# A new order for the last three quarters of the steps of an SSD and SwiGLU kernel

## The chip, the cores and the metric

The kernel runs on one core of a Trainium2 chip. The metric is the device time of one execution in microseconds, the median of several runs. The engines are PE (TensorE; its weight loads are listed apart as PEld), DVE (VectorE), ACT (ScalarE), POOL (GpSimd) and SP (SyncE, which issues most DMAs).

## The reference

A chunked linear attention (Mamba2's SSD) is followed by an RMS norm and a SwiGLU feed-forward network, all in fp32. There are 4 sequences of 768 tokens with 8 heads of width 32 and a state of 16; together they are 3072 tokens of width 256 for the network, whose hidden width is 1536.

```python
for c in range(nc):                                  # chunks of 32
    cum = np.cumsum(la, axis=-1)
    L = np.exp(cum[:, :, :, None] - cum[:, :, None, :]) * causal
    CB = np.einsum('bhin,bhjn->bhij', Cc, Bc)
    y_intra = np.einsum('bhij,bhjd->bhid', CB * L, xc)
    y_inter = np.einsum('bhin,bhnd->bhid', Cc, state) * decay_to_i[:, :, :, None]
    y[:, :, sl] = y_intra + y_inter
    Bx = np.einsum('bhjn,bhjd->bhjnd', Bc, xc) * decay_from_j[:, :, :, None, None]
    state = decay_full[:, :, None, None] * state + np.sum(Bx, axis=2)
...
rms = np.sqrt(np.mean(x * x, axis=-1, keepdims=True) + 1e-06)
xn = x / rms * rms_g
g = xn @ w_gate
silu = g * (1.0 / (1.0 + np.exp(-g)))
return (silu * (xn @ w_val)) @ w_out
```

## The kernel before

**Blocks.** The tokens are worked on in six blocks of 512, numbered 0 to 5. While the network of one block runs on PE, the SSD of the next block is computed between its matmuls. A step's first number is the block in whose stretch it stands; the steps of the SSD in that stretch work for the block after it.

**The network of a block.** Gate and value products are formed by seven products instead of eight (P.1 to P.7, L951 in `product_gv`, for each of six slices j of the hidden width), each of two matmul instructions of 128x256. They are summed up in two PSUM banks, gate and val, of which there are two each. Between them ACT copies the gate bank to SBUF (`take`, L957, tile p), DVE adds such a copy to the value bank (`C`, L963, tile c), ACT takes the silu (`silu`, L208, in place on c, or from gate to u) and DVE or POOL multiplies the halves (`hid` and `hidp`, L976). The product with w_out is a scheme of twenty products (O.0 to O.19, L1072) on sums of hidden tiles (`u` on DVE, `up` on POOL, L1046, tile s); DVE and ACT gather the results into the output tile ob (`w`, L1103 and L1099), and SP stores it (`put`, L1108). Block 0 is simpler: its output product is L983 (step `o`), its results are copied by ACT in `put` (L1114).

**The SSD of the next block.** DVE transposes B and C (`T`, L544), ACT masks them (`Tt`, L1180), PE forms the products CB (`g`, L599), which DVE multiplies with L (`L`, `L1`, L632); L comes from a DMA of log decays, exponentials on ACT (`ex`, L208) and a causal mask on POOL. PE then makes the outputs y (`y`, L736) and the state's additions (L664), DVE updates the states (`S`, L688). For the norm ACT squares y (`sq`) and copies it (`yt`, L804 and L807), PE takes the mean (`ms`, L820), ACT the root by Ln and Exp (`rs`), the roots go out to DRAM and come back on all partitions (`rb`), and DVE scales y to xn (`xn`, L847; `tx`, `txp`: differences for the seven products).

**What sets the order.** The kernel holds one list of 1667 steps, written out as text (from L1269). A loop at its end (L1458 and after) runs through the list and calls the function of each step. Nothing is reordered behind it: each engine executes its own instructions in the order in which the list issues them, and waits where an operand or a buffer isn't ready. Most buffers are few: gate, val, u and L have two each, p and c four, xn, yt, sq and ob one. In PSUM, g shares banks with the output o of block 0.

**Function sets on ACT.** Silu is in one set of functions, Exp and Ln in another. `functions` (L193) remembers the set that the list has loaded last, and emits a load (L200 for silu, L202 for exp and ln) only where a step needs the other one:

```python
        if loaded[0] != name:
            loaded[0] = name
            if name == "silu":
                nc.scalar.preload_act_table(AF.Silu)
            else:
                nc.scalar.preload_act_table_set("natural_log_exp_and_others")
```

A silu, an exponential or a logarithm calls it, and so do two steps by themselves: `table` (silu) and `exps` (exp).

Of the kernel before, what the change touches and what calls it, by code (L numbers as in the profile page):

```python
# [20 lines left out]
def kernel(  # L21
# [35 lines left out]
    P = 128  # L57
    NB, NH, S, D = x.shape
# [5 lines left out]
    T = NB * S  # L64
# [790 lines left out]
    hid = const.tile([P, NF, 2, 256], FP32, name="hid")  # L855
# [383 lines left out]
    def of_chunk(n, fn):  # L1239
# [82 lines left out]
        1:take.6.4 1:P.1.5 1:take.1.5 0:table.0 1:C.11.5 1:P.2.4 1:silu.11.5 1:C.11.4 1:silu.12.2
        1:scale2.1 1:hid.12.2 1:P.7.4 1:P.6.5 1:take.7.4 1:silu.11.4 1:sq2.1.1 1:sq2.0.3 1:sq2.1.2
        2:dT.1 1:P.5.4 1:sq2.0.2 3:bc.1 1:take.6.5 1:two.9 1:Td.0 1:P.4.4 1:hid.11.4 1:sq2.0.0
        1:C.22.4 1:twop.6 1:silu.22.2 1:hid.22.2 1:sq2.0.1 2:dT.0 1:hid.11.5 1:sq2.1.3 1:g
        1:silu.21.4 1:silu.22.4 1:hid.21.4 1:hidp.22.4 1:P.7.5 1:O.15.0 1:P.5.5 1:L1.3 1:L 1:L1.2
        1:u.0 1:take.7.5 1:P.4.5 1:O.2.0 1:O.2.1 1:y.0 1:C.22.5 1:P.3.5 1:silu.21.5 1:w.0 1:hid.21.5
        1:u.1 1:u.2 1:O.15.1 1:O.3.0 1:up.3 1:O.0.0 1:O.0.1 1:up.4 1:O.3.1 1:C.12.5 1:silu.22.5
        1:silu.12.5 2:S.0 1:hid.12.5 1:O.16.0 1:O.6.0 1:O.16.1 1:w.2 1:up.5 1:up.6 1:w.4 1:O.4.0
        1:P.3.4 1:w.10 1:u.9 1:O.4.1 1:O.17.0 1:C.12.4 1:O.9.0 2:T.0.1 1:w.3 1:hid.22.5 1:x.1  # L1330
        1:O.9.1 1:silu.12.4 1:hid.12.4 1:O.17.1 2:Tt.0.0 1:w.12 1:w.5 1:y.1 1:u.10 1:up.11 1:u.7
        1:w.6 1:O.18.0 2:T.1.1 0:exps 2:S.1 1:sq 1:O.13.0 1:O.13.1 1:O.8.0 1:O.8.1 1:w.11 1:w.13
        1:w.20 2:spread.3 2:spread.1 2:sq2.1.0 1:w.16 2:T.1.0 1:yt 1:O.11.0 1:O.18.1 1:w.9 1:ms 1:rs
# [12 lines left out]
        2:take.7.3 2:take.7.2 2:silu.12.1 3:S.0 2:sq2.1.3 2:sq2.0.1 2:spread.0 2:sq2.1.1 3:T.1.1
        2:hid.11.3 2:hid.22.1 2:P.5.2 2:P.5.3 3:Tt.1.1 2:C.22.2 2:C.22.3 2:P.4.3 3:Tt.1.0 3:Td.1
        2:silu.22.3 2:silu.21.3 2:hid.21.3 2:x.1 2:y.1 3:S.1 2:sub.1 2:sq2.0.3 2:hidp.12.1 2:subp.2
        2:P.4.2 2:sq2.0.2 3:dT.0 2:silu.22.2 2:table 2:hidp.22.3 2:sq 2:P.1.5 2:silu.21.2 2:hid.21.2
        1:put.1 3:spread.3 2:P.3.2 3:T.0.0 2:C.12.2 2:take.1.5 2:yt 2:P.3.3 3:T.1.0 3:T.0.1 2:C.12.3  # L1350
        2:hid.22.2 2:P.1.4 2:P.2.5 2:P.6.5 2:silu.12.2 3:Tt.0.1 2:take.1.4 2:silu.12.3 3:Tt.0.0
        2:subp.0 2:hidp.12.3 2:take.6.5 2:hidp.12.2 2:C.11.5 2:P.6.4 2:silu.11.5 3:spread.0 4:dT.0
        2:take.6.4 2:P.2.4 2:C.11.4 2:silu.11.4 3:bc.0 3:subp.0 2:P.7.5 2:take.7.5 2:P.7.4 2:P.5.4
        2:hid.11.5 3:Td.0 2:take.7.4 2:P.4.5 2:C.22.4 2:silu.22.4 2:silu.21.5 2:hid.11.4 2:hid.21.5
        2:P.4.4 2:silu.21.4 2:hid.21.4 3:spread.2 3:subp.2 2:P.5.5 3:sq2.1.3 3:sq2.0.0 3:sq2.0.1
        3:sq2.0.3 3:sq2.1.1 2:ms 2:rs 3:sq2.1.2 2:O.2.0 2:O.15.0 2:hidp.22.4 2:C.22.5 2:P.3.5
        2:C.12.5 2:up.1 2:O.0.0 2:u.2 2:O.2.1 2:O.0.1 2:u.9 2:O.15.1 2:up.0 2:ex.1 2:u.3 2:O.6.0
        2:silu.12.5 2:silu.22.5 2:hid.22.5 2:w.2 2:P.3.4 2:O.16.0 3:sq2.0.2 2:C.12.4 2:w.0
        2:hid.12.5 2:rb 2:xn 2:O.16.1 2:O.3.0 2:w.3 2:O.17.0 2:O.3.1 2:O.4.0 2:O.6.1 2:w.1 2:O.17.1
        2:silu.12.4 2:w.5 2:w.4 2:w.10 3:scale2p.0 2:up.4 2:up.5 3:exps 3:g 3:x.0 2:tx.2 2:txp.0  # L1360
        3:P.1.0 2:tx.1 2:O.9.0 2:O.9.1 2:O.4.1 3:sq2.1.0 2:w.6 2:w.11 2:ex.0 2:exps 3:take.1.0
        3:P.6.0 3:P.2.0 3:C.11.0 2:up.6 2:hidp.12.4 2:up.7 2:w.12 2:O.18.0 2:O.18.1 2:w.9 3:take.6.0
        2:ex.2 2:up.8 2:O.8.0 2:u.10 2:w.7 2:w.13 2:O.8.1 3:P.5.0 2:w.16 2:w.8 3:P.7.0 3:silu.11.0
# [114 lines left out]
```

## Time and profile before

| | |
|---|---|
| median of three runs | 388.94 us (388.43, 388.94, 390.91) |
| span of the profiled execution, the time that its page gives | 387.3 us |
| busy: PE, DVE, ACT, POOL | 381.6, 268.5, 213.6, 149.9 us |
| loads of a function set on ACT | 20 of 1.283 us |
| first instruction that the new order moves | at about 90 us |

Busy time of PE counts a matmul until its modelled end, which lies behind the start of the next one, so a busy share of 99% still leaves room for short waits; the distance between the starts of matmuls, and what the weight loads (PEld) waited for, show these. In a timeline a row is start, length, engine, line, operation, tiles and count; the bracket says how long the engine idled before it, and for whom. "issue" is a wait for nothing that the profile shows.

### The profile page before, as it was taken

The page shows a single profiled execution, that of the slowest core. Times are in us where ns is not written, and L with a number is a line of the kernel's source. Part 1 is how long each engine was busy: PE and PEld are TensorE (multiplying, and loading weights), DVE is VectorE, ACT ScalarE, POOL GpSimd, SP SyncE. Part 2 cuts the span into 40 slices and gives each one's busy share as a digit, 9 for nine tenths or more (in the row PEclk, how much of TensorE's full clock was granted, in tenths as well). Part 3 has the DMA queues.
Part 4 walks back from the last instruction along what each step waited for, and adds up shares of the span by engine and source line. Part 5 has one row for each costly group of instructions (what it writes and reads, how often), then busy time and mean ns, then how long its engine had stood idle before and what let it go on. Part 6 is the DMA issues. An engine that isn't in the chain of part 4 may idle for free.

```text
span 387.3 us, 9593 instructions
## 1 busy us (share of the span) xinstructions
PE 381.6 (99%) x3805; PEld 328.9 (85%) x3805; DVE 268.5 (69%) x593; ACT 213.6 (55%) x451; POOL 149.9 (39%) x168
## 2 busy tenths in 40 slices
PE   8999999999999999999999999999999999999996
PEld 5675488888888989888899988899888899988996
DVE  7886889897636897869475756677474475545674
ACT  3777778978734263578764245742646552245420
POOL 5022145528551463425669401364722046113131
PEclk9999999999999999999999999999999999999999
DMA  7888996588125415534550101001000010000001
GB/s 90 244 129 250 293 192 151 136 134 114 28 67 60 59 50 89 119 54 102 73 96 17 54 15 30 0 16 47 29 3 3 2 34 29 29 1 0 2 0 56
DMA packets 109940, 28.04 MB, mean 72 GB/s; under 512 B 94824, under 2 KB 107848, under 8 KB 109896
## 3 DMA queue, kind: packets, MB, share of 16 engines
q1 hardware_dynamic: 107816, 27.30, 33.8%
q8 instruction: 30, 0.49, 0.6%
q10 hardware_dynamic: 2080, 0.13, 0.4%
q14 instruction: 14, 0.11, 0.1%
HBM read 23.68 MB, written 3.74 MB: 71 GB/s over the span
## 4 chain that ended last, share of the span: by engine, by line
PE 94%; DVE 2%; DMA 2%; issue 1%; ACT 0%; SPq 0%; DVEq 0%
PE gate L951 30%; PE o L1072 23%; PE val L951 22%; PE o L983 5%; PE y L736 3%; PE gate L865 3%; PE g L599 2%; DMA rowe<-e_sb 1%; PE e L460 1%; DMA dT<-rowe 1%; PE gate L875 1%; PE g L592 1%; PE y L664 1%; PE tp L540 1%; PE e L474 0%
## 5 line engine op out<-in xcount | busy, mean ns | idle before, releaser
L963 DVE TENSOR_TENSOR c<-val,p 128x512 f32<-128x512 f32 x99 | 67.3, 688 | 57.5 <-PE val L951 32.7
L957 ACT COPY p<-gate 128x512 f32<-128x512 f32 x99 | 57.2, 582 | 55.6 <-PE gate L951 55.1
L951 PE MATMUL gate<-tx,wgv 128*128 128x256 f32 x264 | 65.9, 381 | 0.0
L976 POOL TENSOR_TENSOR hid<-c 128x256 f32<-128x256 f32 x31 | 24.3, 785 | 94.1 <-ACT c L208 87.5
L208 ACT ACTIVATE c<-c 128x256 f32<-128x256 f32 x99 | 40.6, 416 | 35.8 <-DVE c L963 35.6
L951 PEld LDWEIGHTS gate<-tx,wgv 128*128 128x128 f32 x264 | 49.4, 190 | 7.1 <-issue 0.3
L1072 PE MATMUL o<-two,hid 128*128 128x128 f32 x280 | 38.7, 275 | 0.0
L1103 DVE TENSOR_TENSOR ob<-ob,o 128x128 f32<-128x128 f32 (+1 forms) x90 | 24.0, 299 | 19.9 <-PE o L1072 15.5
L1072 PEld LDWEIGHTS o<-two,hid 128*128 128x128 f32 x280 | 35.6, 192 | 0.7 <-issue 0.2
L976 DVE TENSOR_TENSOR hid<-c 128x256 f32<-128x256 f32 x68 | 30.6, 460 | 7.2 <-ACT c L208 6.8
L951 PE MATMUL val<-tx,sw 128*128 128x256 f32 x132 | 34.0, 382 | 0.0
L951 PE MATMUL val<-xn,sw 128*128 128x256 f32 x132 | 33.6, 381 | 0.1
L951 PE MATMUL val<-xn,wgv 128*128 128x256 f32 x132 | 33.6, 381 | 0.0
L951 PE MATMUL gate<-xn,wgv 128*128 128x256 f32 x132 | 33.2, 381 | 0.0
L951 PE MATMUL gate<-tx,sw 128*128 128x256 f32 x132 | 32.6, 379 | 0.0
L951 PEld LDWEIGHTS val<-tx,sw 128*128 128x128 f32 x132 | 24.6, 190 | 3.9 <-issue 0.4
L951 PEld LDWEIGHTS val<-xn,wgv 128*128 128x128 f32 x132 | 24.8, 190 | 3.4
L208 ACT ACTIVATE u<-gate 128x256 f32<-128x256 f32 (+1 forms) x37 | 14.9, 405 | 22.9 <-PE gate L951 19.3
L951 PEld LDWEIGHTS gate<-tx,sw 128*128 128x128 f32 x132 | 24.8, 190 | 3.2
L951 PEld LDWEIGHTS gate<-xn,wgv 128*128 128x128 f32 x132 | 24.5, 190 | 3.5 <-DVE xn L847 0.2
L951 PEld LDWEIGHTS val<-xn,sw 128*128 128x128 f32 x132 | 24.4, 190 | 3.3 <-DVE c L963 0.2
L1046 POOL TENSOR_TENSOR s<-hid 128x512 f32<-128x512 f32 x13 | 17.3, 1330 | 22.6 <-DVE hid L976 16.2
(202 smaller groups left out, 703.8 us busy)
## 6 DMA issues: line engine op xcount, KB each, us to landing
L<-rowd SPq DMA_DIRECT2D x32, 128.0 KB, 3.3
xr<-in_x_dram SPq DMA_DIRECT2D x24, 128.0 KB, 3.5
out_dram<-ob SPq DMA_DIRECT2D x24, 128.0 KB, 1.8
wr<-in_moe_w_out_dram SPq DMA_DIRECT2D x6, 511.5 KB, 4.9
wr<-in_moe_w_gate_dram SPq DMA_DIRECT2D x5, 511.5 KB, 4.4
wr<-in_moe_w_val_dram SPq DMA_DIRECT2D x5, 511.5 KB, 5.0
br<-in_B_dram SPq DMA_DIRECT2D x23, 64.0 KB, 3.1
dT<-rowe SPq DMA_DIRECT2D x10, 128.0 KB
```

Source lines behind the costliest of these rows:

```text
L208: nc.scalar.activation(**operands)
L599: nc.tensor.matmul(out=g[u, P * i:P * i + P].rearrange("p (t m) -> p t m", t=2), lhsT=T[r, i, 0, u], rhs=T[r, i, 1:3, u], start=(first and ...
L736: nc.tensor.matmul(out=y[2 * k + u][rows, (2 * n + i) * HC:(2 * n + i + 1) * HC], start=(k, u, rows.start) not in opened, stop=True, skip_ ...
L865: nc.tensor.matmul(out=gv[:, k], lhsT=w[:, t, fs], rhs=xns[0][:, t], start=(t == 0), stop=(t == 1))
L951: nc.tensor.matmul(out=dst[:, half[w]], lhsT=lhsT, rhs=rhs, start=(k in (1, 2, 5) and w == 0), stop=True, skip_group_check=True)
L957: nc.scalar.copy(out=t, in_=Xs[j])
L963: nc.vector.tensor_tensor(out=t, in0=Zs[j], in1=a, op=ALU.add)
L976: engine.tensor_tensor(out=hid[:, 2 * j + c // 10 - 1, c % 10 - 1], in0=u, in1=src[:, half[1]], op=ALU.mult)
L983: nc.tensor.matmul(out=o, lhsT=hid[:, f, k // 2, (k % 2) * P:(k % 2 + 1) * P], rhs=wo[:, f], start=opens, stop=(f == NF - 1), skip_group_c ...
L1046: engine.tensor_tensor(out=hidden_or_sum(o), in0=hidden_or_sum(in0), in1=hidden_or_sum(in1), op=ALU.add if in1[0] == "+" else ALU.subtract)
L1072: nc.tensor.matmul(out=Os[blk, b][:, place * P:(place + 1) * P], lhsT=hidden_or_sum(u)[:, g], rhs=rhs, start=(blk, b) not in opened, stop= ...
L1103: nc.vector.tensor_tensor(out=o, in0=o, in1=src, op=ALU.add if what[0] == "+" else ALU.subtract)
```

## The change

From the 400th step on the list is in another order. No step is added or left out. The text of the list becomes one line longer, so lines behind it move by one. The first 399 steps, which prepare the weights and run block 0 up to its network's second half, stay. The diff replaces 131 lines by 132; the first of them are these, with the two places that the order below shows:

```diff
@@ -1307,131 +1307,132 @@
         0:man.16 1:P.2.0 1:C.11.1 1:P.6.1 1:take.6.1 1:P.6.0 1:silu.11.1 1:take.6.0 1:C.11.0
         1:silu.11.0 0:o.5 0:wt.16 1:spread.3 0:sq2.2.1.0 1:sub.3 1:hid.11.1 0:tx.1.3 0:hidgp.22.5
         1:ex.3 0:ex.10 0:sub.8 1:cw.2.1 1:cwp.2.3 1:P.7.0 0:ex.11 1:take.7.0 1:P.5.0 1:C.22.0
-        1:P.7.1 1:P.5.1 1:P.4.0 1:take.7.1 1:twop.1 0:sq2.2.0.3 0:sq2.2.1.1 0:sq2.2.1.2 1:C.22.1
-        1:T.1.1 1:T.0.1 1:P.4.1 1:silu.22.0 1:Tt.1.0 1:silu.21.1 1:bc.1 1:spread.1 1:bc.0
...
-        1:C.22.4 1:twop.6 1:silu.22.2 1:hid.22.2 1:sq2.0.1 2:dT.0 1:hid.11.5 1:sq2.1.3 1:g
...
-        3:P.1.0 2:tx.1 2:O.9.0 2:O.9.1 2:O.4.1 3:sq2.1.0 2:w.6 2:w.11 2:ex.0 2:exps 3:take.1.0
...
+        1:sq2.0.3 1:sq2.0.2 0:put.0 2:bc.0 1:sq2.0.0 1:sq2.1.2 1:spread.1 0:put.2 1:P.3.3 1:P.1.4
+        1:take.1.4 1:g 1:C.12.3 1:silu.12.3 1:hidp.12.3 1:twop.4 1:hidp.12.1 1:twop.7 1:twop.6
...
+        3:P.5.1 3:C.22.1 3:P.1.4 3:silu.22.1 3:hid.22.1 3:P.6.3 3:take.6.3 2:exps 3:take.1.4
+        3:silu.22.0 3:hid.11.1 3:y.1 3:P.2.3 3:hid.11.0 3:sub.3 3:C.11.3 3:P.3.1 3:C.12.1
...
```

PE ahead of the step g that stands in block 1's stretch, in the order before (gate and val are the network's products, o the output of block 0, g the SSD's):

```order
L951 MATMUL gate<-tx,wgv 128x256 x2
L951 MATMUL gate<-tx,sw_992 128x256 x2
L951 MATMUL val<-tx,sw_793 128x256 x2
L951 MATMUL gate<-tx,wgv 128x256 x2
L599 MATMUL g<-T 64x128 x4
```

and now:

```order
L951 MATMUL gate<-tx,wgv 128x256 x4
L983 MATMUL o<-wo,hid 128x256 x4
L951 MATMUL val<-xn,sw_783 128x256 x2
L951 MATMUL gate<-xn,wgv 128x256 x2
L599 MATMUL g<-T 64x128 x4
```

The last matmuls of block 0's output, which stood further ahead, are now four matmuls in front of g.

ACT around the four copies of that output (L1114), before:

```order
L957 COPY p<-gate 128x512
L208 ACTIVATE c<-c 128x256
L1114 COPY ob<-o 128x256 x4
L208 ACTIVATE u<-gate 128x256
L208 ACTIVATE c<-c 128x256
L208 ACTIVATE u<-gate 128x256
```

and now:

```order
L208 ACTIVATE u<-gate 128x256
L957 COPY p<-gate 128x512
L1180 ACTIVATE T<-T,tmask 128x2x128
L208 ACTIVATE c<-c 128x256
L1180 ACTIVATE T<-T,tmask 128x2x128
L1114 COPY ob<-o 128x256 x4
L957 COPY p<-gate 128x512
```

Ahead of the copies there are now two masks, a copy of gate and two silus in a row.

ACT in block 3's stretch, where the step exps of block 2 stands. Before, its load (L202) came ahead of the exponentials of L:

```order
L202 ACT_TABLE_LOAD
L208 ACTIVATE L<-L 128x512
L957 COPY p<-gate 128x512
L1099 COPY ob<-o 128x128
L208 ACTIVATE ob<-o 128x128
L957 COPY p<-gate 128x512
L208 ACTIVATE L<-L 128x512
L200 ACT_TABLE_LOAD
```

and now, where the two exponentials have come earlier and a silu has intervened:

```order
L202 ACT_TABLE_LOAD
L208 ACTIVATE L<-L 128x512 x2
L957 COPY p<-gate 128x512 x2
L200 ACT_TABLE_LOAD
L208 ACTIVATE u<-gate 128x256
L208 ACTIVATE c<-c 128x256 x2
L957 COPY p<-gate 128x512
L208 ACTIVATE c<-c 128x256
L957 COPY p<-gate 128x512
L202 ACT_TABLE_LOAD
L957 COPY p<-gate 128x512
L200 ACT_TABLE_LOAD
```

The step exps loads the exponentials' set once more, and a silu loads its own back behind a single copy; in the whole program the loads are 20 before and 24 now.

243 lines of the change are left out of this document (122 added, 121 removed).

## The prediction

> **What bounds the kernel now.** I read the page's busy line and chain first, then the table by windows, then the waits of PE's weight loads from the place of the change on.
>
> ```profile
> span 387.3 us, 9593 instructions
> PE 381.6 (99%) x3805; PEld 328.9 (85%) x3805; DVE 268.5 (69%) x593; ACT 213.6 (55%) x451; POOL 149.9 (39%) x168
> PE 94%; DVE 2%; DMA 2%; issue 1%; ACT 0%; SPq 0%; DVEq 0%
> ```
>
> PE is busy for 99% of the span and carries 94% of the chain that ended last. The windows say whether that is so stage by stage (columns: length, then busy time and instructions of PE, weight loads, DVE, ACT, POOL, then clock, DMA share and GB/s):
>
> ```profile
> 100.00:120.00 20.00, 20.00 (x94) 17.62 (x93) 9.48 (x20) 8.50 (x20) 8.27 (x10) 1.00 0.31 57
> 340.00:360.00 20.00, 20.00 (x95) 17.60 (x94) 9.50 (x18) 10.51 (x24) 4.37 (x6) 1.00 0.00 0
> ```
>
> In these stretches PE has no idle time, and ACT, the engine on which the change adds something, is busy 8.50 and 10.51 of 20 us. A busy PE can still hide short gaps under the modelled ends of its matmuls, so the stricter view is what the weight loads waited for from 90 us, where the new order begins, to the last matmul (what waited, for whom, us in total, times, longest):
>
> ```profile
> PEld y L736 <- issue: 1.3, 4, 0.3
> PEld ms L820 <- issue: 1.0, 3, 0.3
> PEld o L1072 <- issue: 0.8, 4, 0.2
> PEld g L599 <- issue: 0.7, 2, 0.3
> PEld val L951 <- DVE c L963: 0.6, 2, 0.3
> PEld gate L951 <- issue: 0.5, 3, 0.2
> PEld y L736 <- DVE hid L976: 0.3, 1, 0.3
> PEld o L1072 <- DVE s L1046: 0.3, 1, 0.3
> PEld gate L951 <- DVE xn L847: 0.2, 1, 0.2
> PEld val L951 <- issue: 0.2, 1, 0.2
> ```
>
> The waits on another engine add up to 0.6 + 0.3 + 0.3 + 0.2 = 1.4 us in five places. The issue waits, 1.3 + 1.0 + 0.8 + 0.7 + 0.5 + 0.2 = 4.5 us, stand where PE turns from large matmuls to the small ones of g, y and ms. Nothing waits for a table load or for a DMA. So an order alone can gain at most 1.4 us, 0.4% of the time; what it can lose is open.
>
> **The change part by part.** *PE's own work.* All 1980 matmuls stay, and from 90 us on their shapes are the same in another order: nothing to gain or lose. Turns from one kind of matmul to another are 145 in the order before and 142 now, counted along PE; at up to 0.3 us a turn that is between -0.9 us and 0. I take 0, because most turns are between gate/val and output products, which show almost no issue wait.
>
> *What goes.* The five waits sit at pairs of steps that no longer follow each other in the same way, so I let all of them go: -1.4 us.
>
> *Table loads.* Which function set ACT holds follows from the order of the steps, and a load is emitted only where it differs. Counted along ACT, the old order has 20 loads, the new one 24: not every instruction is kept as it was, four are added.
>
> ```profile
> L202 ACT ACT_TABLE_LOAD x10 | 12.8, 1283 | 0.9 <-PEq L1462 0.8
> L200 ACT ACT_TABLE_LOAD x10 | 12.8, 1283 | 0.2
> 89.09 1.17 ACT L957 COPY p<-gate 128x512 f32<-128x512 f32 x2
> 90.28 1.28 ACT L200 ACT_TABLE_LOAD   x1
> 91.57 0.42 ACT L208 ACTIVATE c<-c 128x256 f32<-128x256 f32 x1
> ```
>
> 4 x 1.283 = 5.13 us more on ACT, which is busy 213.6 of 387 us. What a load costs PE is set by what is queued behind it: the copies of gate (p) that PE needs before it may overwrite the bank, and the silus that DVE's products need. The 20 loads of before stand in the same traffic and no row names one as waited for, so the lower bound is 0; the upper is 5.13. Two of the added loads form a pair with one copy of gate between them (amid block 3's products, where the step exps stands between two takes) and no exponential; there ACT does 1.28 + 0.58 + 1.28 us in a row, and I price what comes through at 0.15 us. At two more places a load now stands directly ahead of the exponentials that a due product needs: an output product whose totals DVE must take first (0.25), and the y of the next block, which waits for L (0.1). Sum 0.5 us, near the lower end, where the 20 rows are.
>
> The row of 90.28 bears on a rule of the Trainium skill, "ScalarE: Activation LUTs", section "What ACT_TABLE_LOAD costs": a load costs about 2.7 us, the drain before it included. By that figure the four loads would be about 10.7 us of ACT. The trace disagrees: the copies end at 89.09 + 1.17 = 90.26, and the silu begins at 91.57, 1.31 us later.
>
> *The place of g.* The step g of block 2 (the small products that feed L) comes earlier and now stands right behind the four copies of the first block's output, which empty the banks g writes into.
>
> ```profile
> 112.92 1.20 ACT L1114 COPY ob<-o 128x256 f32<-128x256 f32 x4 [1.69 <-PE o L983]
> 124.04 1.21 PE L599 MATMUL g<-T 32*64 32x128 f32 x64
> 340.31 1.03 PE L951 MATMUL gate<-tx,wgv 128*128 128x256 f32 x4
> 341.18 1.03 PE L951 MATMUL gate<-xn,wgv 128*128 128x256 f32 x4
> L208 ACT ACTIVATE u<-gate 128x256 f32<-128x256 f32 x33 | 12.5, 382 | 19.4 <-PE gate L951 19.3
> L957 ACT COPY p<-gate 128x512 f32<-128x512 f32 x99 | 57.2, 582 | 55.6 <-PE gate L951 55.1
> L1180 ACT ACTIVATE T<-T,tmask 128x256 f32<-128x256 f32 x16 | 7.5, 500 | 1.2 <-DVE T L544 1.2
> L208 ACT ACTIVATE c<-c 128x256 f32<-128x256 f32 x99 | 40.6, 416 | 35.8 <-DVE c L963 35.6
> ```
>
> Before, the copies ended at 114.12 and g began at 124.04: 9.9 us to spare. In the new order ACT does, from the end of a gate product on, u 0.38, a copy of gate 0.58, two masks 2 x 0.50, a silu 0.42 and the four copies 1.20, plainly 3.58 us; that four copies of 386 ns take 1.20 us shows an overlap of 0.11 at each joint, and five more joints bring it to about 3.0; with some 0.2 us for the start, 3.2. PE has eight matmul instructions to do in that time, at (341.18 - 340.31) / 2 = 0.435 us each 3.5 us. So 0.3 us is left; without the overlaps g would be 0.3 late. I take 0.
>
> *Thin margins.* I went over every place where PE needs a result of another engine in the same manner, in both orders: rows of the chain since its release against 0.435 us for each matmul between. In the old order two places have less than 0.25 us to spare, in the new one about 25. Such a margin holds while DVE takes its usual time, and it doesn't always:
>
> ```profile
> 135.99 1.27 POOL L1046 TENSOR_TENSOR s<-s,hid 128x512 f32<-128x512 f32 x1
> 136.27 1.53 DVE L1046 TENSOR_TENSOR s<-s,hid 128x512 f32<-128x512 f32 x1
> 137.85 0.19 PEld L1072 LDWEIGHTS o<-sw,s 128*128 128x128 f32 x1 [0.32 <-DVE s L1046]
> L1046 DVE TENSOR_TENSOR s<-s,hid x8: 684/692/1535, 136.3 to 375.6; 128x512 f32<-128x512 f32 x8
> L976 DVE TENSOR_TENSOR hid<-c x68: 375/418/948, 60.5 to 369.7; 128x256 f32<-128x256 f32 x68
> L976 DVE TENSOR_TENSOR hid<-c 128x256 f32<-128x256 f32 x68 | 30.6, 460 | 7.2 <-ACT c L208 6.8
> ```
>
> A sum of two SBUF tiles that starts beside a POOL operation took 1.53 us where the median is 0.69, and 0.32 of that reached PE. The products hid have a median of 418 ns and a mean of 460, so an operation of DVE runs 42 ns over on the average: 25 x 42 ns = 1.05 us, of which I let two thirds through, 0.7 us. For places with a wider margin that are hit by a full stretch, as the ones above were, I count two of 0.3 us, 0.6.
>
> *xn and the end.* The first products of blocks 2 to 5 wait for the roots that go out to DRAM and back; from the step ms to them PE now has about as many matmuls or two microseconds more (block 2), so the 0.2 us of xn stays away. The last steps are the same in both orders, so the stretch behind the last matmul is unchanged: 0.
>
> Sum: -1.4 + 0.5 + 0.7 + 0.6 = +0.4 us. The profiled execution has a span of 387.3 us, 1.6 below the median of the three runs, 388.94; the difference goes onto that median: 389.3 us. Both ends: -1.4 us if nothing new waits, and +5.13 on top if all loads come through.
>
> **The rivals.** *All waits go and none comes* (a shade faster): 388.94 - 1.4 = 387.5 us. For it: the margins hold on paper everywhere. Against it: DVE's stretched operations move along with the order and don't vanish; POOL has the same work beside DVE.
>
> *The table loads reach PE* (slower): all four added loads stand ahead of a copy or a silu that PE soon needs, and push it whole: 388.94 + 5.13 = 394.1 us. It decides where ACT's idle time ahead of the load is under 1.28 us. For it: the copies p show 55.1 us of waiting for PE over 99 of them, 0.56 us each, less than a load; the pair has nothing to do with an exponential and lies in the middle of running products. Against it: the 20 loads of before stand between such copies too, and none appears among the waits. By the skill's 2.7 us the same rival would be at about 399.6; the 1.31 us above exclude that.
>
> *The thin margins give way* (slower): of the 25 places half lose the 0.3 us that the three longest waits of before show, 12 x 0.3 = 3.6 us, in place of the 1.3 that I took for stretches: 389.3 - 1.3 + 3.6 = 391.6 us, and with all 25 places 389.3 - 1.3 + 7.5 = 395.5. For it: there are ten times as many such places. Against it: a DVE operation that ran long was the exception among 68.
>
> *The change doesn't do only what its words say*: true for the four loads already, and priced.
>
> **How the numbers follow.** My forecast, 388.6 to 390.4 us, has a chance of 0.55; no waits at all 0.13; thin margins 0.17, a third of it beyond 1%; table loads 0.11; a gain or loss over 1% from something that no row shows 0.02 each. One per cent, 3.9 us, is about what a measurement of this kernel can tell from no change, since the three runs lie 2.5 us apart; the bounds are 385.05 and 392.83. Faster by over 1% has only the last 0.02, as the waits allow 0.4%. Slower: 0.11 + 0.06 + 0.02 = 0.19. Within: 0.79. The range begins at 387.7, which takes in most of the case without waits, and ends at 393.4, which takes in the thin margins up to 18 places and leaves out the table loads in full.
>
> **What would show it.** ACT with 24 loads and 5.1 us more busy time; PE's busy time within 1 us of 381.6. The waits of the weight loads from 90 us on: named engines at 1 to 3 us in total, the issue waits near 4.5. If g L599 waits for ob L1114, the overlap on ACT was overrated; if gate or val waits for p L957 or c L208 right behind a load in five or more places, the loads reach PE; many short waits for DVE's c, s or hid mean that the thin margins give way. A PE total under 380 or a wait of several microseconds for a DMA would make the whole reading wrong.

## The result and the profile after

The new order takes 395.18 us (median of four runs, 394.45 to 396.53) against 389.14 us before (388.43 to 390.91): ratio 1.0157, 95% interval 1.0124 to 1.019. The forecast was 389.3 us and its range ended at 393.4. The profiled span went from 387.3 to 393.5 us, 6.2 us more.

The first matmul of block 0's output (L983), which all kernels here reach by the same instructions, starts anywhere between 68.6 and 70.0 us in the profiles of this study, so spans differ by up to that without any cause in the edit. I therefore compare profiles by the stretch from that matmul to the end of the span: 317.76 us before, 323.80 in the new order, 6.04 more. "The stretch" below is this.

The head of the page after, with the chain, and then one of the two rows of table loads on ACT, from its groups:

```profile
span 393.5 us, 9580 instructions
PE 383.6 (97%) x3805; PEld 328.2 (83%) x3805; DVE 273.5 (70%) x593; ACT 218.1 (55%) x455; POOL 149.9 (38%) x168
PE 85%; DMA 5%; SPq 3%; ACT 2%; DVE 2%; issue 1%; POOL 1%; DVEq 0%; POOLq 0%
```

```profile
L202 ACT ACT_TABLE_LOAD x12 | 15.4, 1283 | 1.0 <-PEq L1463 0.8
```

PE has the same 3805 matmul records. Its share of the chain fell from 94% to 85%, but that isn't a loss of 9%: some of it lies ahead of the change, where the chain now runs over transfers (xr from 11.04 us, 5.98 us long). What PE lost is read from its waits and starts instead. The loads are 24, as counted. What the weight loads waited for from 90 us on (the same view as in the prediction):

```profile
PEld y L736 <- issue: 3.3, 7, 1.3
PEld gate L951 <- ACT p L957: 3.1, 4, 2.2
PEld o L1072 <- issue: 1.6, 6, 0.7
PEld o L1072 <- DVE ob L1103: 1.3, 2, 0.8
PEld ms L820 <- issue: 0.7, 2, 0.3
PEld val L951 <- issue: 0.4, 2, 0.2
PEld g L599 <- ACT ob L1114: 0.3, 1, 0.3
```

Before, no row named p or ob, and the longest single wait was 0.3 us. Now one wait for p is 2.2 us, one for ob 0.8, and one "issue" wait in the y products 1.3. To see what this costs PE, I took for each matmul from 89 us on how much later the next one started than is usual behind that shape (the median for its line and shape). Summed, that is 11.8 us before and 18.0 after, 6.2 us more. The large pieces, with the time at which PE went on:

| us | PE waits for | lost |
|---|---|---|
| 185.28 | p, the copy of gate | 1.96 |
| 206.58 | ob, a total that stands behind xn on DVE | 0.53 |
| 226.54 | L of the y products | 0.29 |
| 272.53 | ob, a total behind a table load on ACT | 0.30 |
| 287.38 | nothing named, within y | 1.38 |
| 327.84 | ob, a total behind hid on DVE | 0.74 |

These six add up to 5.2 us; before, the largest single piece is 0.29. The rest lies in pieces under 0.25 us. Here is the largest, all engines, in the new order:

```profile
179.88 1.03 PE L951 MATMUL gate<-xn,wgv 128*128 128x256 f32 x4
180.74 1.03 PE L951 MATMUL val<-xn,sw 128*128 128x256 f32 x4
181.87 0.69 DVE L963 TENSOR_TENSOR c<-val,p 128x512 f32<-128x512 f32 x1 [0.53 <-PE val L951]
182.48 0.41 DVE L678 TENSOR_TENSOR A<-y,tmask 128x128 f32<-128x128 f32 x2
182.79 0.65 ACT L804 COPY yt<-y 128x256 f32<-128x256 f32 x2 [1.90 <-DVE A L678]
183.45 1.17 ACT L807 COPY yt<-y 64x512 f32<-64x512 f32 x2
184.65 0.58 ACT L957 COPY p<-gate 128x512 f32<-128x512 f32 x1
185.28 2.23 PE L951 MATMUL gate<-tx,sw 128*128 128x256 f32 x8 [1.79 <-ACT p L957]
```

The gate product that is copied to p (P.1.5) begins at 179.88 and is done within about a microsecond. But ACT takes its queue in order, and ahead of that copy stand the four copies yt; these wait for DVE's A (the states' first operation, which reads y too); and A stands on DVE behind a total c that waits for the value product of 180.74. So PE waits for ACT, ACT for DVE, and DVE for PE, and nobody in the chain does anything slowly: 0.69, 0.41, 1.8 and 0.58 us are the usual times. In the order before, take.1.5 stood ahead of yt and the states came earlier.

Of the three waits for ob, only the one at 327.84 us is such a loop: PE's output products, two copies on ACT (0.43 us), a total on DVE (0.29), a hid (0.42) and another total (0.28), then PE again. At 206.58 us the totals stand on DVE behind xn and tx, which began only at 203.41 us, when the roots were back from DRAM. At 272.53 us ACT's copy stands behind one of the added table loads and an exponential:

```profile
269.62 1.28 ACT L202 ACT_TABLE_LOAD   x1
270.91 0.63 ACT L208 ACTIVATE L<-L 128x512 f32<-128x512 f32 x1
271.45 0.25 ACT L1099 COPY ob<-o 128x128 f32<-128x128 f32 x1
271.73 1.33 DVE L1103 TENSOR_TENSOR ob<-ob,o 128x128 f32<-128x128 f32 x4 [0.39 <-ACT ob L1099]
```

### The profile page after: what moved, and what is told of

Its sections match the earlier page's. It is cut to its first block, busy times and chain, and to the rows that moved or that the text cites. A ratio compares the mean times of both kernels' runs of the same rounds, so it can differ in the third digit from the quotient of the medians.

```text
span 393.5 us, 9580 instructions
## 1 busy us (share of the span) xinstructions
PE 383.6 (97%) x3805; PEld 328.2 (83%) x3805; DVE 273.5 (70%) x593; ACT 218.1 (55%) x455; POOL 149.9 (38%) x168
## 4 chain that ended last, share of the span: by engine, by line
PE 85%; DMA 5%; SPq 3%; ACT 2%; DVE 2%; issue 1%; POOL 1%; DVEq 0%; POOLq 0%
PE gate L951 28%; PE val L951 21%; PE o L1072 20%; PE o L983 5%; PE y L736 3%; PE gate L865 3%; DMA xr<-in_x_dram 2%; PE g L599 1%; SPq L143 1%; DMA roots<-r 1%; DMA rowe<-e_sb 1%; PE gate L875 1%; DMA dT<-rowe 1%; PE y L664 1%; DMA sq<-roots 1%
## 5 line engine op out<-in xcount | busy, mean ns | idle before, releaser
L208 ACT ACTIVATE c<-c 128x256 f32<-128x256 f32 x99 | 39.2, 414 | 31.4 <-DVE c L963 31.1
L976 DVE TENSOR_TENSOR hid<-c 128x256 f32<-128x256 f32 x68 | 32.0, 484 | 8.8 <-ACT c L208 8.8
```

Of the source, the lines that this page charges most:

```text
L208: nc.scalar.activation(**operands)
L976: engine.tensor_tensor(out=hid[:, 2 * j + c // 10 - 1, c % 10 - 1], in0=u, in1=src[:, half[1]], op=ALU.mult)
```

## The experiments

Theory A: the loss comes from such chains through two or three queues, and at 286 us from PE running out of code (so far a guess, from a transfer of the instruction queue that begins there). Theory B: the four added table loads reach PE.

**e1: without the useless pair of loads.**

```diff
-        3:P.5.1 3:C.22.1 3:P.1.4 3:silu.22.1 3:hid.22.1 3:P.6.3 3:take.6.3 2:exps 3:take.1.4
+        3:P.5.1 3:C.22.1 3:P.1.4 3:silu.22.1 3:hid.22.1 3:P.6.3 3:take.6.3 3:take.1.4
```

> The new order without the step exps of block 2, so without the pair of table loads that has only a copy of gate between (22 loads, ACT 2 x 1.283 us less busy). Theory A (the loss comes from chains in which a product of PE is waited for by DVE, DVE by ACT and ACT by PE again, at 184, 207, 273 and 328 us, and from a halt of PE in the y products at 286 us): the span stays within 0.3 us of 393.5 and the wait at 184 us for the copy p stays near 2 us. Theory B (the added table loads reach PE): the span falls by up to 2.6 us, to 390.9.

395.24 us (394.8 to 395.38), ratio to before 1.016 (1.0133 to 1.0186); span 393.1, stretch 323.82, so 0.02 us longer than with the pair. The wait for p stays at 2.2 us. The sum hides two differences that are not the edit's: 0.42 us less at 205 to 207 us, ahead of it, and a halt that is 0.35 us longer. Set matmul against matmul (the starts of the same records in both profiles), the two keep their distance to 0.06 us from 212 to 284 us, with the pair at 232 us between. So these two loads, with 2.6 us of ACT, cost nothing in the new order, and for them B fails.

**e2: the copy of gate ahead of yt.**

```diff
-        2:silu.12.3 2:hidp.12.3 2:P.4.2 2:silu.21.2 2:hid.21.2 2:P.1.5 2:P.3.2 2:C.12.2 3:S.0 2:yt
-        2:table 2:take.1.5 2:silu.12.2 2:hidp.12.2 2:hidp.22.3 3:spread.3 2:sq2.0.1 2:spread.2
+        2:silu.12.3 2:hidp.12.3 2:P.4.2 2:silu.21.2 2:hid.21.2 2:P.1.5 2:P.3.2 2:C.12.2 3:S.0 2:take.1.5 2:yt
+        2:table 2:silu.12.2 2:hidp.12.2 2:hidp.22.3 3:spread.3 2:sq2.0.1 2:spread.2
```

> The new order with one step moved: the copy of gate take.1.5 of block 2 stands ahead of the four copies yt instead of behind them. Theory A: the wait of PE at 184 us, 1.96 us in the starts of the matmuls, goes, and the span falls by about 2 us to 391.5, with the other waits as they were. Theory B: nothing moves by more than 0.3 us, since all 24 loads are kept.

393.5 us (393.43 to 395.41), ratio 1.0129 (1.0095 to 1.0163); span 391.8, stretch 322.99, 0.81 us shorter with all 24 loads kept, where 2 were expected (the other 0.9 us of the span lie ahead of the change). The wait at the first product went, but the row for p is still there:

```profile
PEld gate L951 <- ACT p L957: 2.5, 3, 1.9
```

It is the next copy, take.1.4, which still stands behind yt. The starts of the matmuls show 1.71 us lost there instead of 1.96; the wait for ob at 206 us halved to 0.28, as it did in e1, where nothing was changed ahead of it, so that part is not the edit's. Matmul against matmul the edit's own place gained 0.49 us. The wait moved to the next copy in the same queue.

**e3: y.0 and y.1 apart.**

```diff
-        4:silu.22.1 4:hidp.22.1 3:txp.3 4:P.7.0 4:take.7.0 4:C.11.0 4:Td.1 4:y.0 4:y.1 4:yt 4:P.5.0
-        4:C.22.0 4:P.4.1 4:silu.21.1 4:hid.21.1 4:P.3.1 4:C.12.1 4:P.4.0 4:silu.22.0 4:hidp.22.0
+        4:silu.22.1 4:hidp.22.1 3:txp.3 4:P.7.0 4:take.7.0 4:C.11.0 4:Td.1 4:y.0 4:P.5.0
+        4:C.22.0 4:P.4.1 4:silu.21.1 4:hid.21.1 4:P.3.1 4:y.1 4:yt 4:C.12.1 4:P.4.0 4:silu.22.0 4:hidp.22.0
```

> The new order with y.1 and yt of block 4 moved behind three gate and value products, so that y.0 and y.1 no longer stand back to back. Theory A1 (the halt of 1.38 us at 286 us is PE running out of code, since a transfer of the instruction queue begins at 285.1 us in the middle of the many short products): with 12 long matmul records, 2.6 us, between, the halt goes and the span falls by about 1.3 us to 392.2. Theory A2 (the halt is a wait for data of y.1 that the profile does not name): it goes too if the data comes within 2.6 us, but the instruction transfer then lies elsewhere; told apart by where the transfer begins and whether PE halts there. Theory B: no change of more than 0.3 us.

395.24 us (394.8 to 395.67), ratio 1.0163 (1.0131 to 1.0195); span 393.4, stretch 324.45, 0.65 us longer. PE's timeline in the new order, and then in e3, shows why:

```profile
285.77 0.43 PE L736 MATMUL y<-L,xr 64*32 64x64 f32 x26
287.38 0.64 PE L736 MATMUL y<-L,xr 64*32 64x64 f32 x38 [1.17 <-issue]
```

```profile
287.75 0.86 PE L736 MATMUL y<-L,xr 64*32 64x64 f32 x64
293.20 0.43 PE L820 MATMUL ms<-sq,mean 128*32 128x128 f32 x8 [1.80 <-POOL sq L788]
```

The halt after 26 of 64 records is gone, as A1 says, though the span did not fall to the 392.2 forecast; the instruction transfer began at 284.43 us, among long products, and PE did not stop. But yt and the squares came later with y.1, and ms, which stayed where it was, now waited 1.8 us for POOL's sum of them. I had not followed what stands behind y.1.

**e4: four totals earlier.**

```diff
-        2:O.16.1 2:O.17.1 2:O.4.1 2:silu.12.4 2:w.3 2:xn 2:tx.2 2:txp.0 3:P.1.0 3:P.2.0 2:w.5 2:w.6
-        2:w.4 2:w.10 2:O.9.0 2:O.18.0 2:up.6 2:O.8.0 2:O.8.1 2:O.18.1 2:O.9.1 2:hid.22.5 2:hidp.12.4
+        2:O.16.1 2:O.17.1 2:O.4.1 2:silu.12.4 2:w.3 2:w.4 2:w.10 2:xn 2:tx.2 2:txp.0 3:P.1.0 3:P.2.0 2:w.5 2:w.6
+        2:O.9.0 2:O.18.0 2:up.6 2:O.8.0 2:O.8.1 2:O.18.1 2:O.9.1 2:hid.22.5 2:hidp.12.4
...
-        3:u.14 3:up.15 3:txp.1 3:ex.2 4:P.1.1 3:w.12 3:ex.1 4:take.1.1 3:w.20 3:w.16 3:w.8 3:w.15
+        3:u.14 3:up.15 3:txp.1 3:w.12 3:ex.2 4:P.1.1 3:ex.1 4:take.1.1 3:w.20 3:w.16 3:w.8 3:w.15
...
-        4:w.3 4:w.5 4:u.11 4:w.13 4:O.11.0 4:O.11.1 4:hid.12.4 4:w.16 4:O.5.0 4:u.7 4:up.8 4:O.13.0
+        4:u.11 4:w.16 4:w.3 4:w.5 4:w.13 4:O.11.0 4:O.11.1 4:hid.12.4 4:O.5.0 4:u.7 4:up.8 4:O.13.0
```

> The new order with four totals of the output product moved ahead: w.4 and w.10 of block 2 ahead of xn, w.12 of block 3 ahead of the exponentials with their table load, w.16 of block 4 ahead of w.3. Theory A: the waits of PE for ob at 207 (0.53), 273 (0.30) and 328 us (0.74 and some 0.25 behind it) go, and the span falls by 1.5 to 1.8 us to about 391.8. Theory B: only the wait at 273 us, behind a table load, has to do with a load; 0.3 us at most.

396.5 us (396.0 to 397.98), ratio 1.02 (1.0166 to 1.0234); span 394.3, stretch 325.09, 1.29 us longer. Two waits for ob went, and two others took their place:

```profile
PEld gate L951 <- DVE xn L847: 1.5, 1, 1.5
PEld o L1072 <- DVE hid L1046: 1.0, 1, 1.0
```

On DVE w.10 now stood ahead of xn and held it up; and once O.5 went early, the next product waited for u.7, which was still behind hid.12.4. The halt in the y products was 1.76 us here, 0.38 more. The wait at 272.53 us went when its total stood ahead of the load (0.29 us, matmul against matmul). A total that is moved ahead delays what it is moved past.

**e5: the states earlier, take.1.5 left behind yt.**

```diff
-        2:hid.11.2 2:P.4.3 2:silu.21.3 2:hid.21.3 2:P.5.2 2:C.22.2 2:P.3.3 3:Tt.1.1 2:C.12.3
-        2:silu.12.3 2:hidp.12.3 2:P.4.2 2:silu.21.2 2:hid.21.2 2:P.1.5 2:P.3.2 2:C.12.2 3:S.0 2:yt
+        2:hid.11.2 2:P.4.3 2:silu.21.3 2:hid.21.3 2:P.5.2 2:C.22.2 2:P.3.3 3:Tt.1.1 3:S.0 2:C.12.3
+        2:silu.12.3 2:hidp.12.3 2:P.4.2 2:silu.21.2 2:hid.21.2 2:P.1.5 2:P.3.2 2:C.12.2 2:yt
```

> The new order with one step moved in another place of the same chain: the states S.0 ahead of block 2's yt now come before the total C.12.3 instead of behind C.12.2, which waits for a product of PE; take.1.5 stays behind the four copies yt. Theory A (the wait at 184 us is the chain product, DVE total, DVE states, ACT copies yt, ACT take.1.5, PE; moving only take.1.5 left 1.7 us because take.1.4 behind yt then came late): the wait goes at both products, and the span falls by about 2 us to 391.5. Rival A' (the four copies yt, 1.75 us, are by themselves too long ahead of a take): at least 1 us of the wait stays.

394.32 us (393.32 to 395.77), ratio 1.0139 (1.0108 to 1.0169); span 393.3, stretch 323.37, 0.43 us shorter. The wait for p at 184 us went (1.96 to under 0.2 us). In its place DVE, with the states' 1.3 us ahead of C.12.3, was late with hid.21.2, 0.97 us, so the place gained 0.84 us, matmul against matmul; and the halt in the y products grew from 1.38 to 2.09 us. The link is shown; little of the time is won.

**e6: y apart and ms later.** The edit of e3, and

```diff
-        4:silu.11.0 4:hid.11.0 4:hid.11.1 4:ms 4:P.1.3 4:P.2.3 4:take.1.3 4:C.11.3 4:silu.11.3
-        4:C.12.0 4:silu.12.0 4:P.6.2 4:take.6.2 4:P.6.3 4:take.6.3 4:P.2.2 4:P.5.3 4:P.7.2
+        4:silu.11.0 4:hid.11.0 4:hid.11.1 4:P.1.3 4:P.2.3 4:take.1.3 4:C.11.3 4:silu.11.3
+        4:C.12.0 4:silu.12.0 4:P.6.2 4:take.6.2 4:P.6.3 4:take.6.3 4:P.2.2 4:ms 4:P.5.3 4:P.7.2
```

> The new order with y.0 and y.1 of block 4 apart as in the run before, and the mean ms, which then waited 1.8 us for POOL's sum of squares, five products later (its result is used much later). Theory A1 (code): no halt in the y products, no wait at ms, span 393.5 - 1.4 = 392.1. Rival A2 (something else holds PE there for the 1.4 us in either case): the span stays within 0.3 us of 393.5, with the wait in a third place.

395.06 us (394.41 to 396.19), ratio 1.0158 (1.0136 to 1.018); span 394.4, stretch 325.82. The granted clock was 0.995 here (0.83 from 180 to 190 us): eight matmul records between 185 and 188.5 us took twice their time, 1.7 us, so 324.1 without that. Neither the halt nor the wait of ms came, but a third, 1.66 us, after which PE went on at 294 us: yt (1.8 us) and three squares stood on ACT ahead of a silu whose result PE needed. The span did not fall, as rival A2 had said, so this run can't tell the two apart; in e14 the halt is gone and nothing has taken its place.

**e7: all moves together**, with the totals in a second version (the edits of e5 and e6, w.12 as in e4, and these):

```diff
+        2:O.16.1 2:O.17.1 2:O.4.1 2:silu.12.4 2:w.3 2:xn 2:tx.2 2:txp.0 3:P.1.0 3:P.2.0 2:w.4 2:w.10 2:w.5 2:w.6
...
+        4:O.9.1 4:u.10 4:up.5 4:O.4.1 4:O.16.1 4:O.17.1 4:O.6.1 4:silu.12.4 4:u.6 4:hid.12.4 4:u.11 4:O.8.0 4:O.8.1 4:w.16 4:u.7
+        4:w.3 4:w.5 4:w.13 4:O.11.0 4:O.11.1 4:O.5.0 4:up.8 4:O.13.0
```

> The new order, still with 24 table loads, with the moves of the two runs before, and the totals in a second version: w.4 and w.10 of block 2 just ahead of w.5 (behind xn), w.12 of block 3 ahead of the exponentials, and in block 4 on DVE hid.12.4 and u.11 ahead of O.8, w.16 and u.7 right behind it. Theory A: the waits at 184, 207, 273, 286 and 328 us, 1.96 + 0.53 + 0.30 + 1.38 + 0.74 = 4.9 us, go, and the span is 388.6, 1.3 us above that of the order before. Theory B (loads): whatever goes there, 2 us or more of the 6.2 stay beside it, and the span stays over 390.

393.48 us (392.85 to 394.24), ratio 1.0115 (1.0095 to 1.0135); span 392.4, stretch 322.52: 1.28 us shorter, not 4.9. At 328 us nothing is left. What is left are the two new waits of e5 and e6 (0.97 and 1.65) and 0.27 and 0.38 us for ob. The sign set for theory B, a span that stays over 390, came true as well; but the waits that are left are for hid and ob, and e10 to e14 take most of them away with every load in place.

**e8: the chain put into the order before.**

```diff
-        2:silu.22.3 2:silu.21.3 2:hid.21.3 2:x.1 2:y.1 3:S.1 2:sub.1 2:sq2.0.3 2:hidp.12.1 2:subp.2
+        2:silu.22.3 2:silu.21.3 2:hid.21.3 2:x.1 2:y.1 2:sub.1 2:sq2.0.3 2:hidp.12.1 2:subp.2
...
-        1:put.1 3:spread.3 2:P.3.2 3:T.0.0 2:C.12.2 2:take.1.5 2:yt 2:P.3.3 3:T.1.0 3:T.0.1 2:C.12.3
+        1:put.1 3:spread.3 2:P.3.2 3:T.0.0 2:C.12.2 3:S.1 2:yt 2:take.1.5 2:P.3.3 3:T.1.0 3:T.0.1 2:C.12.3
```

> The order before, with the chain of the new one put in: in block 2 the states S.1 behind the total C.12.2, and take.1.5 behind yt. Theory A: from that product's end DVE's total 0.69, the states' first operations 0.41, the copies 1.8 and take 0.58 stand against three products of 0.86, so PE now waits for p there for 1 to 1.5 us, and the span of 387.3 becomes 388.3 to 388.8. Theory B: nothing is changed at the loads, so nothing over 0.3 us.

390.25 us (389.72 to 393.74), ratio 1.0054 (1.0031 to 1.0076); span 388.4, stretch 319.27, 1.51 us longer than before, as expected; 1.46 of them arise at the edit, matmul against matmul. Its waits have a row that the order before has not:

```profile
PEld gate L951 <- ACT p L957: 1.7, 2, 1.3
```

**e9: four table loads put into the order before.**

```diff
-        3:C.11.3 3:silu.11.3 3:P.5.1 3:P.6.3 3:take.6.3 3:P.6.4 3:C.22.1 3:hid.11.0 3:silu.22.1
+        3:C.11.3 3:silu.11.3 3:P.5.1 3:P.6.3 2:exps 3:take.6.3 3:P.6.4 3:C.22.1 3:hid.11.0 3:silu.22.1
...
-        4:take.1.4 4:P.2.5 4:P.6.5 4:P.6.4 4:P.2.4 4:take.6.5 4:P.7.5 4:take.6.4 4:hid.12.3 4:C.11.5
+        4:take.1.4 4:P.2.5 4:P.6.5 4:P.6.4 4:P.2.4 4:take.6.5 4:P.7.5 3:exps 4:take.6.4 4:hid.12.3 4:C.11.5
```

> The order before with four more table loads and nothing else: the step exps put ahead of two takes, in block 3 (ahead of take.6.3) and block 4 (ahead of take.6.4), so that each time a load of the exponentials' set, a copy of gate and a load of silu's stand in a row, as in the new order. Theory A (the loads lie in ACT's idle time): 24 loads, 5.1 us more busy on ACT, the span within 0.4 us of 387.3. Theory B (loads reach PE): the span rises by 2 to 5 us, with PE waiting for p or c right behind the loads.

391.28 us (391.02 to 391.91), ratio 1.0066 (1.0041 to 1.0091); span 389.5, stretch 320.07, 2.31 us longer: here B is right. Matmul against matmul the two pairs cost 1.14 and 1.03 us; 0.15 us is a longer wait for xn at 153 us, ahead of them. The first pair, from the timeline:

```profile
227.43 1.28 ACT L202 ACT_TABLE_LOAD   x1
228.73 0.59 ACT L957 COPY p<-gate 128x512 f32<-128x512 f32 x1
229.33 1.28 ACT L200 ACT_TABLE_LOAD   x1
230.62 0.42 ACT L208 ACTIVATE c<-c 128x256 f32<-128x256 f32 x1
230.95 0.57 ACT L957 COPY p<-gate 128x512 f32<-128x512 f32 x1
231.56 0.73 PEld L951 LDWEIGHTS gate<-tx,wgv 128*128 128x128 f32 x4 [0.61 <-ACT p L957]
233.89 0.73 PEld L951 LDWEIGHTS val<-xn,sw 128*128 128x128 f32 x4 [0.67 <-DVE c L963]
```

ACT is busy from 227.43 to 231.5 without a gap; the copy that PE waits for is behind the second load, and the delay reappears two products later by way of DVE's total. So a load has no price of its own: in the new order a pair cost nothing, here a pair costs 1.0 to 1.1 us.

**e10: second moves** (against e7):

```diff
+        2:silu.12.3 2:hidp.12.3 2:P.4.2 2:silu.21.2 2:hid.21.2 3:S.0 2:P.1.5 2:P.3.2 2:C.12.2 2:yt
...
+        4:C.22.0 4:P.4.1 4:silu.21.1 4:hid.21.1 4:P.3.1 4:y.1 4:C.12.1 4:P.4.0 4:silu.22.0 4:hidp.22.0
+        4:silu.11.1 4:silu.21.0 4:hid.21.0 4:silu.12.1 4:hidp.12.1 4:P.3.0 4:P.1.2 4:take.1.2
+        4:silu.11.0 4:yt 4:hid.11.0 4:hid.11.1 4:P.1.3 4:P.2.3 4:take.1.3 4:C.11.3 4:silu.11.3
+        4:C.12.0 4:silu.12.0 4:P.6.2 4:take.6.2 4:sq 4:P.6.3 4:take.6.3 4:P.2.2 4:P.5.3 4:P.7.2
...
+        4:hidp.22.3 4:P.5.2 4:ms 4:C.22.2 4:P.4.2 4:silu.21.2 4:hid.21.2 4:P.3.3 4:P.4.3 4:silu.21.3
```

> The kernel with all moves, corrected at the two places where a new wait had come up: the states S.0 of block 2 now behind hid.21.2 (ahead of it they held up a hidden product for 0.97 us), and in block 4 yt and sq behind the silu and hid.21.0 that PE waits for (1.65 us). Still 24 table loads. Theory A (each wait is a chain through DVE's and ACT's queues, and goes where the queue is in the right order): both waits go and the span falls from 392.4 to 389.8 or less. Rival A' (ACT and DVE are simply too busy in these stretches, so a wait taken away comes back behind the next product): the span stays over 391.5.

392.34 us (392.13 to 393.17), ratio 1.0094 (1.0072 to 1.0116); span 390.8, between the two forecasts; stretch 321.71, 2.09 us shorter than in the new order. Both old waits went; yt on ACT now held up other copies of gate, 0.75 us at 183 and 0.90 + 0.50 us at 293 and 295 us.

**e11: two swaps at the waits of the order before.**

```diff
-        1:P.3.4 1:w.10 1:u.9 1:O.4.1 1:O.17.0 1:C.12.4 1:O.9.0 2:T.0.1 1:w.3 1:hid.22.5 1:x.1
+        1:P.3.4 1:u.9 1:w.10 1:O.4.1 1:O.17.0 1:C.12.4 1:O.9.0 2:T.0.1 1:w.3 1:hid.22.5 1:x.1
...
-        2:P.2.0 2:silu.11.1 2:hid.11.1 1:tx.3 2:scale2.0 2:C.11.0 2:P.5.1 2:L1.3 2:take.6.1 1:txp.2
+        2:P.2.0 2:silu.11.1 2:hid.11.1 1:tx.3 2:C.11.0 2:scale2.0 2:P.5.1 2:L1.3 2:take.6.1 1:txp.2
```

> The order before with two swaps at its own waits: u.9 of block 1 ahead of w.10 (so that DVE's sum is not behind a total that waits for ACT; 0.30 us of PE), and in block 2 the total C.11.0 ahead of scale2.0 (0.1 us). Theory A: both waits go, the span falls by 0.3 to 0.4 us to 386.9; in the times that is 0.1%, at the edge of what can be seen. If w.10 then comes late for the next output product, nothing is won.

387.9 us (387.09 to 388.93, twelve runs) against 388.86 for the order before, ratio 0.9977 (0.9964 to 0.9991); span 387.0, stretch 317.02, 0.74 us shorter. It is the fastest kernel of the study. The 0.30 us at 137 us and the 0.1 us at 161 us are gone; so is the 0.17 us for xn at 153 us, which varies from profile to profile.

**e12: y earlier in the order before**, so that an instruction transfer falls within it.

```diff
-        4:C.12.0 4:P.3.1 4:C.12.1 4:silu.12.0 4:P.1.2 4:take.1.2 4:P.1.3 4:P.2.3 4:silu.12.1
+        4:C.12.0 4:P.3.1 4:C.12.1 4:silu.12.0 4:P.1.2 4:take.1.2 4:P.1.3 4:y.0 4:y.1 4:P.2.3 4:silu.12.1
...
-        4:P.6.3 4:take.6.3 4:y.0 4:y.1 4:P.7.2 4:C.11.2 4:silu.11.2 4:hid.11.3 4:P.5.2 4:P.7.3 4:sq
+        4:P.6.3 4:take.6.3 4:P.7.2 4:C.11.2 4:silu.11.2 4:hid.11.3 4:P.5.2 4:P.7.3 4:sq
```

> The order before with y.0 and y.1 of block 4 moved four products earlier, ahead of P.2.3, to where the instruction queue's transfer began (286.9 us). Their operands are there since 285.3 us. Theory A1 (PE runs out of code when such a transfer begins inside the short y products: about 2.3 us pass from its beginning until PE goes on, and some 80 of the short products, 1.1 us, are left till then): the transfer begins within the y products, PE halts there for 1.0 to 1.4 us with nothing named as waited for, and the span rises from 387.3 to 388.3 or 388.7. Theory A2 (the halt in the new order was a wait for data): no halt here, span within 0.3 us of 387.3.

389.62 us (389.15 to 390.48), ratio 1.0021 (1.0007 to 1.0035); span 388.4, stretch 319.30, 1.54 us longer. The halt came, with nothing named:

```profile
288.78 0.27 PE L736 MATMUL y<-T,S 32*64 32x64 f32 x2 [0.51 <-issue]
```

It costs 0.72 us in the starts, less than the 1.0 forecast. The transfer began 0.3 us ahead of the y products rather than inside them, which may be why. Another 0.5 us is a longer wait for xn at 153 us, ahead of the edit and no effect of it, and 0.3 us comes in small pieces behind the y products.

**e13: third moves** (against e10): yt behind the copies of gate that PE needs, in block 2 and in block 4.

```diff
+        2:silu.12.3 2:hidp.12.3 2:P.4.2 2:silu.21.2 2:hid.21.2 3:S.0 2:P.1.5 2:P.3.2 2:C.12.2 2:P.1.4 2:take.1.5 2:take.1.4 2:yt
...
+        4:take.7.2 4:C.11.2 4:hid.11.3 4:P.7.3 4:take.7.3 4:yt 4:hid.12.0 4:C.22.3 4:silu.22.3
...
+        4:silu.11.2 4:C.12.3 4:hid.21.3 4:sq 4:P.3.2 4:C.12.2 4:silu.12.3 4:hid.12.3 4:P.1.5 4:take.1.5 4:ms
```

> The kernel of the second moves, with the copies yt once more later: in block 2 behind take.1.5 and take.1.4, in block 4 behind take.7.3, with sq and ms later too. Still 24 table loads. Theory A (each wait is a matter of the order in ACT's queue): the waits for p at 182 us (0.75 and 0.13) and at 292 us (0.90 and 0.50) go without another coming up, and the span falls from 390.8 to 388.5 or 389, 1.2 to 1.7 us above the order before. Rival A' (ACT is too full in these stretches): at least 1 us of the 2.3 comes back behind the next product, and the span stays at 389.8 or above.

391.68 us (391.12 to 392.75), ratio 1.0074 (1.0046 to 1.0102); span 390.0, stretch 320.97, 2.83 us shorter than in the new order. The waits at 183 and 293 us are gone but for 0.34 us at 186; with the squares later, ms waited again, 1.59 us until 303 us. By its span, over 389.8, and by that wait, this run went the way of rival A'; e14 tests whether it is ACT's load or the place of ms.

**e14: ms seven products later** (against e13).

```diff
-        4:silu.11.2 4:C.12.3 4:hid.21.3 4:sq 4:P.3.2 4:C.12.2 4:silu.12.3 4:hid.12.3 4:P.1.5 4:take.1.5 4:ms
+        4:silu.11.2 4:C.12.3 4:hid.21.3 4:sq 4:P.3.2 4:C.12.2 4:silu.12.3 4:hid.12.3 4:P.1.5 4:take.1.5
...
-        4:take.6.5 4:P.6.4 4:take.6.4 4:P.2.4 4:C.11.4 4:P.7.5 4:take.7.5 4:P.7.4 4:take.7.4
+        4:take.6.5 4:P.6.4 4:take.6.4 4:P.2.4 4:C.11.4 4:P.7.5 4:take.7.5 4:P.7.4 4:take.7.4 4:ms
```

> The kernel of the third moves with one step more: the mean ms of block 4 stands seven products later, so that it no longer waits 1.6 us for POOL's sum of squares; its result is used far later. Still 24 table loads. Theory A: that wait goes and no other takes its place, the span falls from 390.0 to 388.4, 1.1 us above the order before. Rival A' (a wait taken away comes back behind the next product, since ACT, DVE and POOL are too full): 1 us or more comes back, the span stays at 389.4 or above.

390.73 us (390.07 to 390.97), ratio 1.0048 (1.003 to 1.0066); span 388.8, stretch 319.49. The windows of the new order (first fence) and of e14 (second), columns as in the prediction:

```profile
170.00:200.00 30.00, 28.21 (x206) 23.55 (x205) 17.70 (x38) 21.41 (x47) 11.39 (x12) 1.00 0.42 88
270.00:300.00 30.00, 28.69 (x343) 24.66 (x342) 15.65 (x36) 15.96 (x33) 13.90 (x17) 1.00 0.06 19
```

```profile
170.00:200.00 30.00, 29.83 (x224) 25.54 (x223) 18.28 (x39) 21.88 (x48) 12.35 (x13) 1.00 0.43 96
270.00:300.00 30.00, 30.00 (x336) 25.77 (x336) 15.52 (x34) 14.46 (x31) 10.72 (x15) 1.00 0.06 19
```

ACT has about the same work in both, 21.4 and 21.9 us in the first stretch, 16.0 and 14.5 in the second, and PE goes from 28.2 to 29.8 and from 28.7 to 30.0 of 30 us. So the engines were not too full (A' fails); their queues were in the wrong order. Moves alone took back 323.80 - 319.49 = 4.3 of the 6.0 us, with all 24 loads in place. The remaining 1.7 us lie in pieces of 0.34 us and less; whether loads have a part in them stays open, since this order was not run without them.

## Why the prediction was wrong

*What bounds the kernel; what goes; g; the end.* These held. PE is still the engine that sets the time, and an order alone could gain little. The waits of before are gone but for one of 0.2 us for c. The g behind the four copies shows 0.3 us on its weight load, now put down to ob, as I had named it for a sign that the overlap was overrated; but it waited the same 0.3 us before, as "issue", and no matmul is late, so the 0 held. No wait for xn came up on PE itself, but one came through the totals behind xn in DVE's queue (207 us).

*Thin margins: the step that failed.* "I went over every place where PE needs a result of another engine in the same manner, in both orders: rows of the chain since its release against 0.435 us for each matmul between." I counted the rows on the engine that hands over to PE, from the product that releases the result. At 185 us that product is the gate product itself, and by this count the copy had time enough. I did not ask when the instruction ahead of it in ACT's queue could run, and what that one waits for on DVE, and that one again on PE. Through all queues the chain is 0.69 + 0.41 + 1.8 + 0.58 us and a few handovers, 3.5 us from the value product's end (181.77) to 185.28, against two products of PE, 1.7 us, and the profile shows 1.96 us lost. The wait for ob at 328 us, 0.74 us, is of the same kind (PE, ACT, DVE, PE), and the one at 207 us, 0.53 us there and 0.28 in other profiles, comes of totals behind xn in DVE's queue. So the term of 0.7 us should have been about 3.2, and my list of 25 thin places had not the thick ones on it. The rival in which the margins give way had the right side and too small a size, 391.6 us; and its reason, DVE operations that run long beside POOL, is not what happened: in the chain at 185 us DVE's total took its usual 0.69.

*PE's own work.* I took 0 for the issue waits, from the number of turns between kinds of matmuls. They rose from 4.5 to 3.3 + 1.6 + 0.7 + 0.4 + 0.2 = 6.2 us, and one of them, the halt in the y products, cost 1.38 us in the starts. The turns did not cause it; the runs tie it to where an instruction transfer falls among them (last section). That was outside my list of rivals.

*Table loads.* The count was right, ACT is 4.5 us busier, and the cost stayed near the lower end: the pair that I had put at 0.15 us costs 0.0 in e1, and the output product behind a load, put at 0.25, lost 0.30 us (at 272.53). For the y products, put at 0.1, the chain to the 0.29 us at 226.54 runs over POOL and DVE, not over a load. But the reason I gave, that no row of before names a load as waited for, was weaker than I thought: in the order before, two pairs at other places cost 2.2 us (e9), and even there the rows name only p and c, the operations behind the loads.

*The signs.* Three of them failed: the waits for named engines add up to 6.3 us instead of 1 to 3, the issue waits to 6.2 instead of 4.5, and PE's busy time rose by 2.0 us, where it was to stay within 1 us. Why the same matmuls count as busier is open; of the 6.0 us, the pieces under 0.25 us are not explained one by one.

*The range.* It gave a fifth of the chance to slower by over 1%, nearly all of it by way of the loads or the stretched operations. Both the mechanisms that did it were missing, so the width came from the wrong things.

## What to carry to other kernels

When a kernel with in-order queues and a saturated engine is reordered, follow each result that the saturated engine needs back through the instruction ahead of it in each queue until you come to that engine again, and set the whole loop against the work in between; a margin counted on one engine hides the loop. A move that removes a wait delays what it is moved past, so read the trace again after each one: here it took four rounds to win back 4.3 us. A busy share of 55% on an engine says nothing about whether its queue holds up another.

## What the runs showed of the hardware

PE stopped beside transfers of code. The page of the new order lists for one instruction queue (packets, MB, share):

```profile
q8 instruction: 30, 0.49, 0.5%
```

That is 16 KB for each. I take it for PE's: PE's 7610 matmul and weight-load records make 254 for each of the 30 transfers, about 64 bytes a record. In long products they go unnoticed: in the order before, 23 of them begin from 90 us on, and no wait with nothing named is longer than 0.3 us. In six profiles where one began among the short y products of block 4, or just ahead of them, PE stopped, with "issue" as the only reason, and went on 2.25 to 2.62 us after the transfer's beginning:

| kernel | transfer begins | PE goes on | between |
|---|---|---|---|
| new order | 285.10 | 287.38 | 2.28 |
| e1 | 284.57 | 286.93 | 2.36 |
| e2 | 283.42 | 285.67 | 2.25 |
| e4 | 285.57 | 287.92 | 2.35 |
| e5 | 284.55 | 287.17 | 2.62 |
| e12 | 286.31 | 288.78 | 2.47 |

In all but the last the stop is behind the same record, the 26th of the second y<-L,xr. A wait for data is unlikely: in the new order no operation of DVE, ACT or POOL ends between 286.30 and 287.38 us, and from 284 to 288 us the only transfers that begin are of instructions. The transfer itself takes only 0.9 to 1.3 us; what fills the rest was not tried.

A transfer among short products is not enough, though. In e5 one begins at 231.00 us among the y products of block 3 (230.75 to 232.18 us), and in the new order one at 135.58 us, 0.9 us ahead of those of block 1; behind neither do two matmuls start more than 0.32 us apart. What decides between the two cases is open; that PE runs out of code fits the six stops but is not shown.

The Trainium skill ("Runtime: NRT & Kernel Launch", section "Instruction fetch mechanics") says that code is refilled in blocks of 16 KiB, which are 256 instructions, and that the cost of crossing a block's boundary is "mostly hidden". The sizes agree with the trace; if the stops are such crossings, they cost 0.7 to 2.1 us in these six profiles.
